# Exponentials of three heads on ScalarE, of the fourth on VectorE as weighted 16-bit linear pieces; a new normalization and out-projection

## The chip, the cores and the metric

The kernel runs on one core of a Trainium2 chip. The metric is the device time of one execution in microseconds (us), lower is better. Each quoted time is a median of several runs. Runs of one kernel that lie over 1.5% above its fastest are set apart as slow, and only fast runs are compared.

The engines are TensorE (PE in the profile, PEld for its weight loads), VectorE (DVE), ScalarE (ACT), GpSimd (POOL) and SyncE (SP), which issues the DMAs. PEclk is the clock granted to TensorE as a fraction of full speed. In the traces it has two values only, 0.5 and 1.0. It changes on a grid of 3.41 us. The Trainium skill, "TensorE: Matmul & The Clock Gate", Part 1: The HAM clock gate, says the same: two states, half and full rate, set by how busy TensorE has been, in windows of 3413 ns.

## The reference

Four layers on 2,048 tokens of width 512. Layers 1 and 3 are a local dilated attention, not touched by the change. Layers 2 and 4 are full attention with 32 query heads of 16 dimensions that share one key and one value head. Cut to what matters:

```python
# x: (1, 2048, 512); H = 32 heads, Dh = 16
q = (x @ wq).reshape(B, S, H, Dh).transpose(0, 2, 1, 3)
k = x @ wk                      # one key head for all
v = x @ wv
scores = einsum("bhqd,bkd->bhqk", q, k) * Dh ** -0.5
p = softmax(scores)             # 2 layers x 32 heads x 2048 x 2048 exponentials
o = einsum("bhqk,bkd->bhqd", p, v)
out = o.transpose(...).reshape(B, S, H * Dh) @ wo
```

## The kernel before

The work of a full-attention layer is cut into chunks: one head, 128 keys, 512 queries. There are 2,048 chunks in a layer, 4,096 in all. Three chunks make a tile. For each tile TensorE computes three score matmuls, ScalarE takes one exponential over 128x1536, and TensorE multiplies the result with the values (PV).

```python
def emit_scores(i):                                   # L498
    for n, (qc, t, a, kt, g) in enumerate(cs):        # cs: three chunks
        nc.tensor.matmul(st[:, n, :], lhsT=KAB[32*g:32*g+32, a, kt*128:(kt+1)*128],
                         rhs=QT[32*g:32*g+32, t, qc*512:(qc+1)*512],
                         start=True, stop=True, tile_position=(32*g, 0))     # L503
def emit_exp(i):
    nc.scalar.activation(out=pt[...], in_=st[...], func=AF.Exp, scale=scale) # L511
def emit_pv(i):
    ...
        nc.tensor.matmul(o_ps[...][32*g:32*g+32, :], lhsT=VE[:, kt, :], rhs=pt[:, n, :],
                         start=(kt == 0), stop=(kt == NT-1),
                         tile_position=(0, 32*g))                            # L547
```

A score matmul uses 32 rows of the array (its contraction is 32 long), and a PV matmul uses all 128 rows and 32 columns. So consecutive groups use different tilings of the array. A group of matmuls in different row groups or column groups runs at nearly the same time (in the traces they start within 10 ns of each other); I call that one stream.

VE holds the values with a column of ones beside them, so a PV matmul also sums the exponentials. When the 16 key tiles of a block (four heads, 512 queries) are done, VectorE copies the block out, spreads the sums with a shuffle, takes a 128x512 reciprocal and multiplies; four output matmuls and four additions follow for every block.

```python
def finish_block(qc, t, a):
    nc.vector.tensor_copy(out=ot[:], in_=ops[:])
    nc.vector.stream_shuffle(out=lb[:, sl], in_=ot[:, sl], mask=[16] * 32)   # L535
    nc.vector.reciprocal(out=lb[:, sl], in_=lb[:, sl])                       # L536
    nc.vector.tensor_tensor(out=onb[:, sl], in0=ot[:, sl], in1=lb[:, sl], op=ALU.mult)
    ...  # later, four times: y = onb x wo_pad (L520), x_sb += y (L521)
```

## Time and profile before

| | before |
|---|---|
| median time, as known before the result | 2388.58 us (3 runs, 2383.91 to 2392.66) |
| from first to last exponential, two attention stages | 955.2 + 956.3 us |
| ScalarE busy in attention | 97% |
| one exponential of 128x1536, start to start | 1.331 us median, 1.40 us mean |
| granted TensorE clock in attention | 0.50 |
| VectorE busy in attention | 25 to 32% |

The page of the profile shows the span in 40 slices, each digit being the busy share of a slice in tenths; PEclk is the granted clock in tenths. These are the rows of TensorE, ScalarE and the clock in the kernel before.

```profile
PE   5887899999999999999877879999999989999996
...
ACT  5314999999999999999842169999999999999996
...
PEclk9998555555555555555589975555555555555555
```

The two attention stages are the two long stretches in which ScalarE shows 9. In both of them the clock is 5, half speed. The costliest groups of the kernel before are next. Each line gives source line, engine, operation, result and operands, shapes and count, then busy time in us, the mean of one in ns, and the idle time before them with the engine that ended it.

```profile
L511 ACT ACTIVATE pt<-st 128x1536 bf16<-128x1536 f32 (+1 forms) x1366 | 1860.7, 1508 | 63.9 <-PE st L503 62.0
L503 PE MATMUL st<-QT,KAB 32*128 32x512 bf16 x4096 | 859.4, 597 | 176.1 <-ACT pt L511 168.2
L547 PE MATMUL o_ps<-pt,VE 128*32 128x512 bf16 x4096 | 864.7, 607 | 1.4 <-ACT pt L511 1.0
...
L536 DVE RECIPROCAL lb<-lb 128x512 f32<-128x512 f32 (+1 forms) x70 | 214.9, 3075 | 2.1
```

ScalarE is busy 1,861 us with exponentials and idle only 64 us before them: it bounds these stages. Before score matmuls TensorE waits 168 us for ScalarE; ScalarE waits 62 us for TensorE. (One exponential is listed at 1.5 us, but consecutive ones overlap and start 1.33 us apart.) The busy time by stretches of time (columns: busy us of PE, PEld, DVE, ACT, POOL with counts, then PEclk, DMA share, GB/s) gives the shares in a steady part of attention.

```profile
300.00:400.00 100.00, 91.22 (x446) 21.76 (x444) 26.36 (x30) 97.25 (x73) 0.00 (x0) 0.50 0.00 1
```

In 100 us there are 73 exponentials. The PE column, 91%, is not the array at its peak: it contains the latency of each group. The timeline of the same kernel (columns: start us, duration us, instruction, count) shows how often groups can follow each other.

```profile
901.34 0.61 PE L547 MATMUL o_ps<-pt,VE 128*32 128x512 bf16 x3
901.52 2.79 ACT L511 ACTIVATE pt<-st 128x1536 bf16<-128x1536 f32 x2 [0.17 <-PE st L503]
...
901.89 0.61 PE L503 MATMUL st<-QT,KAB 32*128 32x512 bf16 x3
...
902.43 0.61 PE L547 MATMUL o_ps<-pt,VE 128*32 128x512 bf16 x3
```

PV group, score group and PV group start 0.54 to 0.55 us apart, so the two groups of a tile take 1.09 of ScalarE's 1.33 us at half clock. TensorE has little to spare there.

### The profile page before, as it was taken

To read this page: it belongs to the slowest core of one execution; us is meant where nothing else is said; L and a number is where in the kernel's file an instruction comes from. 1 tells how busy PE (TensorE), PEld (TensorE's weight loads), DVE (VectorE), ACT (ScalarE), POOL (GpSimd) and SP (SyncE) were. 2 spreads that over 40 slices of the span, in tenths; PEclk is the share of its full clock that TensorE was granted. 3 is DMA by queue.
4 is the path that set the end of the run, shared out by engine and by line. 5 is a ranking of instruction groups with operands and counts; after the bars stand their busy time and mean duration, and the time that the engine had idled before them with its cause. 6 is when DMAs were issued, how large, how long until landed. Compare 5 with 4: busy or idle time off the path is not lost.

```text
span 2389.7 us, 27720 instructions
## 1 busy us (share of the span) xinstructions
PE 2085.2 (87%) x11652; PEld 611.5 (26%) x11652; DVE 839.2 (35%) x1061; ACT 2015.7 (84%) x1603; POOL 35.7 (1%) x67
## 2 busy tenths in 40 slices
PE   5887899999999999999877879999999989999996
PEld 5433222222222222222153332222222222222221
DVE  3875222232223222322339832222222222222222
ACT  5314999999999999999842169999999999999996
POOL 1002000000000000000010000000000000000000
PEclk9998555555555555555589975555555555555555
DMA  1101000000000000000000000000000000000000
GB/s 63 37 2 28 1 1 1 1 1 1 1 1 1 1 1 1 1 1 1 1 3 2 1 1 1 1 1 9 1 1 1 1 10 1 1 9 1 1 1 11
DMA packets 14315, 11.56 MB, mean 5 GB/s; under 512 B 7904, under 2 KB 13536, under 8 KB 14048
## 3 DMA queue, kind: packets, MB, share of 16 engines
q1 hardware_dynamic: 13120, 8.60, 1.4%
q8 instruction: 95, 1.56, 0.3%
q10 hardware_dynamic: 1056, 1.05, 0.1%
q14 instruction: 44, 0.36, 0.1%
HBM read 7.37 MB, written 2.10 MB: 4 GB/s over the span
## 4 chain that ended last, share of the span: by engine, by line
ACT 39%; PE 31%; issue 17%; DVE 12%; POOL 0%; DMA 0%; ACTq 0%; SPq 0%; DVEq 0%; POOLq 0%
ACT pt L511 38%; PE st L503 11%; PE o_ps L547 8%; PE y L520 6%; DVE lb L536 3%; PE ps L184 3%; DVE prod L209 2%; PE y L265 1%; PE ps L359 1%; DVE pv L253 1%; PE acc L256 1%; DVE ot L528 1%; DVE lb L535 1%; DVE onb L537 1%; DVE qsq L373 0%
## 5 line engine op out<-in xcount | busy, mean ns | idle before, releaser
L511 ACT ACTIVATE pt<-st 128x1536 bf16<-128x1536 f32 (+1 forms) x1366 | 1860.7, 1508 | 63.9 <-PE st L503 62.0
L503 PE MATMUL st<-QT,KAB 32*128 32x512 bf16 x4096 | 859.4, 597 | 176.1 <-ACT pt L511 168.2
L547 PE MATMUL o_ps<-pt,VE 128*32 128x512 bf16 x4096 | 864.7, 607 | 1.4 <-ACT pt L511 1.0
L528 DVE COPY ot<-o_ps 128x512 f32<-128x512 f32 x64 | 44.3, 692 | 1163.2 <-PE o_ps L547 1163.2
L503 PEld LDWEIGHTS <-KAB 32*128 32x128 bf16 x4096 | 236.5, 99 | 766.1 <-issue 764.0
L547 PEld LDWEIGHTS <-VE 128*32 128x32 bf16 x4096 | 154.4, 101 | 621.4 <-issue 621.3
L521 DVE TENSOR_TENSOR x_sb<-x_sb,y 128x512 f32<-128x512 f32 x256 | 176.1, 688 | 226.1 <-PE y L520 226.1
L536 DVE RECIPROCAL lb<-lb 128x512 f32<-128x512 f32 (+1 forms) x70 | 214.9, 3075 | 2.1
L520 PE MATMUL y<-wo_pad,onb 128*128 128x512 bf16 x256 | 155.3, 607 | 20.6 <-DVE onb L537 12.3
L89 ACT ACTIVATE xn<-x_sb,ln_nmr,ln_rstd 128x512 bf16<-128x512 f32 x44 | 33.3, 806 | 92.0 <-DVE ln_nmr L83 88.8
L209 DVE TENSOR_TENSOR prod<-Qch,Kch 128x4096 bf16<-128x4096 bf16 x32 | 72.4, 2279 | 58.1 <-ACT Kch L188 56.7
L184 PE MATMUL ps<-xnT,w_sb 128*32 128x512 bf16 x1536 | 90.7, 392 | 1.9 <-ACT Vch L188 1.9
L184 PEld LDWEIGHTS <-w_sb 128*32 128x32 bf16 x1536 | 80.1, 141 | 12.1 <-issue 7.5
L256 PE MATMUL acc<-pv,ident 128*128 128x512 bf16 x256 | 68.7, 402 | 15.9 <-DVE pv L253 10.3
L212 PE MATMUL lg<-prod,ident 128*128 128x512 bf16 x256 | 60.6, 379 | 18.8 <-DVE prod L209 18.8
L258 ACT CAST Och<-acc 128x2048 bf16<-128x2048 f32 x8 | 14.9, 1866 | 72.2 <-PE acc L256 72.2
L253 DVE TENSOR_TENSOR pv<-attn,Vch 128x2048 bf16<-128x2048 bf16 x64 | 73.2, 1222 | 1.5 <-PE acc L256 1.5
L214 ACT ACTIVATE L<-lg 128x512 f32<-128x512 f32 x16 | 9.6, 598 | 70.7 <-PE lg L212 70.7
L99 PE MATMUL pT<-ident,xn 128*128 128x128 bf16 x256 | 27.6, 256 | 44.6 <-ACT xn L89 29.8
L520 PEld LDWEIGHTS <-onb 128*128 128x128 bf16 x256 | 26.4, 103 | 131.6 <-issue 89.7
L535 DVE STREAM_SHUFFLE lb<-ot 128x512 f32<-128x512 f32 (+1 forms) x70 | 46.8, 673 | 0.0
L537 DVE TENSOR_TENSOR onb<-ot,lb 128x512 bf16<-128x512 f32 (+1 forms) x70 | 44.6, 641 | 2.1
(89 smaller groups left out, 538.8 us busy)
## 6 DMA issues: line engine op xcount, KB each, us to landing
xi<-in_A_x_dram SPq DMA_DIRECT2D x4, 512.0 KB, 5.6
wo_r_73<-in_A_wo_dram SPq DMA_DIRECT2D x4, 512.0 KB, 8.2
w_sb<-in_A_wqkv_dram SPq DMA_DIRECT2D x4, 384.0 KB, 8.2
out_dram<-xo SPq DMA_DIRECT2D x2, 512.0 KB, 3.0
out_dram<-xo ACTq DMA_DIRECT2D x2, 512.0 KB, 4.9
wq_sb<-in_B_wq_dram SPq DMA_DIRECT2D x4, 128.0 KB, 3.2
woB_sb<-in_B_wo_dram SPq DMA_DIRECT2D x4, 128.0 KB, 3.7
wo_pad<-in_B_wo_dram SPq DMA_DIRECT2D x16, 32.0 KB, 1.8
```

The source lines that it names most:

```text
L184: nc.tensor.matmul(ps[32 * c:32 * c + 32, :], lhsT=wqkvP[:, kt, j, d, :], rhs=xnT[:, kt, c * 512:(c + 1) * 512], start=(kt == 0), stop=(kt ...
L209: nc.vector.tensor_tensor(out=prod[:], in0=Q[:, dsl, :], in1=K[:, dsl, PAD - DIL * w:PAD - DIL * w + 512], op=ALU.mult)
L253: nc.vector.tensor_tensor(out=pv[:], in0=attn[:, w, :].unsqueeze(1).to_broadcast([PCH, DG, 512]), in1=V[:, ds_, PAD - DIL * w:PAD - DIL * ...
L256: nc.tensor.matmul(acc[:, i, :], lhsT=ident[:PCH, :PCH], rhs=pv[:, i, :], start=(w == 0), stop=(w == W - 1))
L503: nc.tensor.matmul(st[:, n, :], lhsT=KAB[32 * g:32 * g + 32, a, kt * 128:(kt + 1) * 128], rhs=QT[32 * g:32 * g + 32, t, qc * 512:(qc + 1) ...
L511: nc.scalar.activation(out=pt[:, :len(cs), :], in_=st_tiles[i][:, :len(cs), :], func=AF.Exp, scale=scale)
L520: nc.tensor.matmul(y[:], lhsT=onb[:, cols], rhs=wo_pad[:, t, a, :], start=True, stop=True)
L521: nc.vector.tensor_tensor(out=x_sb[:, qt, :], in0=x_sb[:, qt, :], in1=y[:], op=ALU.add)
L535: nc.vector.stream_shuffle(out=lb[:, sl], in_=ot[:, sl], mask=[16] * 32)
L536: nc.vector.reciprocal(out=lb[:, sl], in_=lb[:, sl])
L537: nc.vector.tensor_tensor(out=onb[:, sl], in0=ot[:, sl], in1=lb[:, sl], op=ALU.mult)
L547: nc.tensor.matmul(o_ps[(qc, t, a)][32 * g:32 * g + 32, :], lhsT=VE[:, kt, :], rhs=pt[:, n, :], start=(kt == 0), stop=(kt == NT - 1), tile ...
```

## The change

The intent is to take a quarter of the exponentials off ScalarE. A step is now one key tile for four heads (1,024 steps). Three heads go through the exponential of ScalarE as before. The fourth head, a different one in each key tile, goes to VectorE:

- A first instruction (L523, "fix") turns its scores from PSUM into 16-bit integers, scaled so that the integer is a logarithm to the base 2.
- A bfloat16 number whose bits are taken as an integer is nearly a logarithm of its value: adding a constant and reading the integer's bits as bfloat16 gives 2 to that power, with straight pieces between the powers. One such curve is a coarse exponential. Four copies, shifted by about a quarter of a power each and added with weights, are a finer one.
- Each copy is one 16-bit pass of VectorE over four key tiles at once (L528), so one pass per step. The weighted sum costs VectorE nothing: PE makes it, with four weighted copies of the values. PV rises from 4 to 7 matmuls a step.

The normalization goes too. The sums of two blocks are gathered by DMA into 128x32, VectorE takes one small reciprocal, DMAs spread it through DRAM, and GpSimd multiplies (L582). Two blocks are packed so that the output projection is four matmuls and one addition for each 128 queries, done once per 512 queries, where it had been done once per block. Not shown below: the bound on the scores up to which this fast path is taken falls from 50 to 42 (`SAFE_EXP_ARG`). The diff, cut to its core (cuts marked with ...):

```diff
+J_OFF = (-0.375, 31.125, 62.875, 95.375)
+J_W = (1.0, 0.84375, 0.71875, 0.60546875)
+T_SCALE = 512.0 * 1.4426950408889634 * DH ** -0.5
+T_BIAS = -1057.4609391288138
...
-    VE = big.tile([128, NT, 32], BF16, name="VE")
+    VE = big.tile([128, NT, NJ, 32], BF16, name="VE")     # values times J_W[j]
...
+    dvp = ctx.enter_context(tc.tile_pool(name=f"Bf_dv_{tag}", bufs=1, space=PSUM))
...
+    def emit_scores(s):                                   # gd = kt % 4 goes to VectorE
+        st = st_tiles[s] = stp.tile([128, 3, 512], F32, name="st")
+        dv = dv_tiles[s] = dvp.tile([128, 512], F32, name="dv")
...
+    def emit_fix(s):
+        nc.vector.tensor_scalar(out=t_tiles[m][:, r, :], in0=dv_tiles.pop(s)[:], scalar1=T_SCALE,
+                                scalar2=T_BIAS, op0=ALU.mult, op1=ALU.add)
+    def emit_pass(m, j):
+        nc.vector.tensor_scalar(out=it[:].bitcast(I16), in0=t_tiles[m][:], scalar1=0.25,
+                                scalar2=127.0 * 128.0 + J_OFF[j], op0=ALU.mult, op1=ALU.add)
+    def emit_pv_act(s):       # three matmuls with VE[:, kt, 0, :]
+    def emit_pv_dve(m, j):    # four matmuls, heads r at key tiles kt0 + r, with VE[:, kt, j, :]
...
-        nc.vector.stream_shuffle(...); nc.vector.reciprocal(lb 128x512); nc.vector.tensor_tensor(onb)
+        nc.sync.dma_start(out=S2[32*g:32*g+32, a, :], in_=src[32*g+16:32*g+17, :])   # 4 times
+        nc.vector.reciprocal(out=S2[:], in_=S2[:])                                   # 128x32
+        rd (DRAM) <- S2 (4 DMAs), lb <- rd broadcast (8 DMAs)
+        nc.gpsimd.tensor_tensor(out=onc[qc][:, t, :], in0=X[:], in1=lb[:], op=ALU.mult)
```

The score of the fourth head has one PSUM bank (`bufs=1`): the next one can't be computed before VectorE has converted the last.

## The prediction

> **What bounds it now.** The two attention stages run from 230 to 1198 us and from 1414 us to the end, about 1,940 of 2,390 us (timeline). In them ScalarE is 97% busy (busy time by 100-us windows): 1,366 exponentials of 128x1536 take 1,860.7 us (costliest groups), one per 1.34 us in steady state. TensorE waits for it, but not by much: a group of three score or PV matmuls occupies 0.54 us from start to start (timeline), of which I take 0.43 us as streaming and 0.11 us as the change between the two tilings; so 1.09 of 1.34 us. Its granted clock is 0.50 through both stages. VectorE is 28% busy.
>
> **What changes.** Per step (one key tile, four heads; 1,024 steps):
> - ScalarE: one 1536-wide exponential instead of 1.33. Floor 1,024 x 1.345 = 1,377 us, 460 us less than 1,366 x 1.345.
> - VectorE: one PSUM conversion of 128x512 (the 512-wide PSUM copy took 0.69 us) and one 16-bit pass over 2,048 elements. No pass of that form is in the trace; a 16-bit copy of 512 took 0.29 us, which fits the 4x rate that the Trainium skill, "VectorE: DVE Perf Modes", The perf-mode tier table, gives for 16-bit tensor_scalar in SBUF. Estimate: 0.69 us. Back-to-back instructions overlap by about 0.07 us, so 1.25 to 1.38 us. The 3.35-us reciprocals and three quarters of the output additions go. Per-block copies and additions bring VectorE to about 1,400 us: level with ScalarE.
> - TensorE: PV rises from 4 to 7 matmuls a step. I counted the compiled order: the fourth head's score is one matmul into a single PSUM bank, and in more than a third of the steps it sits among the PV matmuls. That gives 2.8 changes of tiling and 4.0 serial streams a step: 2.04 us at clock 0.5, but 1.18 us at full clock. **The clock decides.**
>
> **The clock.** Attention streams about 64% of the time at clock 0.5 and never leaves it. Elsewhere (granted clock in 3.4-us windows) dense matmuls raise it after one full window, VectorE-bound stretches at about 56 to 75% of full-clock streaming keep it, and windows under 40% lose it. The change streams about 85% at half clock, then about 59% at full clock: I expect it to rise and mostly stay, with drops at block ends. The shakiest step.
>
> **Sum.** Outside attention: 450 us, plus about 6 for the extra V copies. Attention at full clock: ScalarE, VectorE and the single-buffered PSUM bank (score, convert, score) couple to about 1.45 us a step, 1,485 us; block ends (copy, four output matmuls, the pause of PV) about 40; two tails through four DMA hops, about 12 us each, little more than now. About 2,005 us; some stretches at half clock make it 2,030. Fully at half clock it would be about 2,600.
>
> Predicted **2030 us, 1930 to 2270**. Faster by over 2%: 0.83; within 2%: 0.04; slower: 0.13.
>
> **What would show it.** Right: exponentials x1024 at about 1.5 us mean duration, ScalarE still over 88% busy in attention; VectorE over 85% busy, passes near 0.69 us; granted clock mostly 1.0 in attention; PV matmuls x7168. Wrong on the clock: 0.5 throughout, TensorE near 100% busy, ScalarE idle before exponentials waiting on scores, steps near 2 us. Wrong on VectorE: passes of 1.2 us or more, ScalarE waiting while VectorE is full.
>
> **What would make it wrong.** A low clock; passes off the 4x rate; the single PSUM bank turning every VectorE delay into a TensorE stall.

## The result, and the profile after

| | before | after |
|---|---|---|
| median, fast runs | 2386.57 us (4 runs, 2383.91 to 2392.66) | 1968.18 us (4 runs, 1960.04 to 1973.17) |
| ratio | | 0.824 (95% interval 0.822 to 0.827) |
| first to last exponential, both stages | 1911.5 us | 1470.9 us |
| the rest of the span | 478.2 us | 487.4 us |
| mean granted clock | 0.583 | 0.971 |

A ratio, here and below, is the mean time of one kernel's fast runs over that of the other's in the same rounds, so it isn't quite the ratio of the medians. The last three rows are of the profiled runs (spans 2389.7 and 1958.3 us). The gain of 431 us between those two is 441 us won in the attention stages and 9 us lost around them.

The rows of the page that answer to those of before:

```profile
PE   5888799999999999989678888999999999999995
...
DVE  4797589999999999999638966999999999999995
ACT  5232599999999999999652236999999999999994
...
PEclk9999799999999999999889997999999999999998
```

ScalarE and VectorE are now both at 9 in attention, and the clock is 9 (nearly full) instead of 5. The groups after:

```profile
L517 ACT ACTIVATE pt<-st 128x1536 bf16<-128x1536 f32 x1024 | 1413.8, 1461 | 69.8 <-PE st L511 42.6
L523 DVE TENSOR_SCALAR tt<-dv 128x512 int16<-128x512 f32 x1024 | 700.8, 684 | 107.3 <-PE dv L511 96.2
L528 DVE TENSOR_SCALAR it<-tt 128x2048 int16<-128x2048 int16 x1024 | 699.6, 700 | 7.4
L536 PE MATMUL o_ps<-it,VE 128*32 128x512 bf16 x4096 | 648.0, 387 | 1.7 <-DVE it L528 1.5
L536 PE MATMUL o_ps<-pt,VE 128*32 128x512 bf16 x3072 | 513.9, 393 | 1.8 <-DVE xo L595 0.7
L511 PE MATMUL st<-QT,KAB 32*128 32x512 bf16 x3072 | 434.8, 390 | 32.3 <-ACT pt L517 26.2
```

The exponentials fell from 1,861 to 1,414 us of busy time, and they still wait only 70 us. The 16-bit pass takes 0.70 us for four times the elements that the fix handles in 0.68 us. A matmul now lasts 0.39 us where it had lasted 0.60 us. The busy time by stretches, first in the steady part and then at the start of the first attention stage:

```profile
300.00:400.00 100.00, 94.41 (x792) 21.44 (x788) 93.53 (x151) 98.51 (x73) 2.54 (x2) 1.00 0.05 10
...
236.00:244.00 8.00, 8.00 (x46) 1.34 (x39) 5.63 (x9) 5.54 (x5) 0.00 (x0) 0.50 0.00 0
244.00:250.00 6.00, 5.55 (x53) 1.42 (x47) 4.44 (x8) 5.76 (x5) 0.00 (x0) 0.87 0.00 1
250.00:260.00 10.00, 8.66 (x74) 2.19 (x74) 8.17 (x14) 10.00 (x8) 0.00 (x0) 1.00 0.01 2
```

From 236 to 244 us the clock is still 0.50: TensorE is busy all 8 us, ScalarE 5.5 of 8, and exponentials come about every 2.07 us (in the timeline four steps lie between the starts at 235.36 and 243.62 us). From 245 us the clock is full, and ScalarE is full too. After that, the first stage has a single 3.4-us window at half clock (at 655 us) and the second, full from 1218 us on, has none until its end. So the start of each stage, before the clock rises 18 to 24 us after the first exponential, shows what a whole stage would be without it. The first four steps are short (1.36 us), because the PV matmuls of VectorE's pieces begin only at 233.0 and 1199.9 us; after them, nine steps of the second stage (1199.83 to 1217.54 us) took 1.97 us each in the mean. Over both stages the exponentials start 1.436 us apart on average and 1.348 us in the median.

One visible disturbance is left in steady state, in the timeline of the kernel after:

```profile
430.30 1.27 POOL L582 TENSOR_TENSOR onc<-X,lb 128x512 bf16<-128x512 f32 x1 [42.11 <-DMA lb<-rd]
430.43 1.68 DVE L528 TENSOR_SCALAR it<-tt 128x2048 int16<-128x2048 int16 x1
...
434.11 2.79 ACT L517 ACTIVATE pt<-st 128x1536 bf16<-128x1536 f32 x2 [0.83 <-PE st L511]
```

While GpSimd multiplies, the VectorE pass takes 1.68 instead of 0.70 us, and shortly after ScalarE waits 0.83 us. The Trainium skill, "SBUF — State Buffer", Who interferes with whom, says that a VectorE copy or tensor_scalar in a two-port mode and a GpSimd instruction lock the shared pair of SBUF ports against each other for a whole instruction. This trace agrees: the pass ends 0.54 us after GpSimd's instruction, nearly a whole pass later. It is so for the whole trace: of 24 passes that started during one of the 32 products, 23 ended 0.55 us after it, and the 11 fixes that started during one, which read PSUM, took their usual 0.68 to 0.69 us.

### The profile page after: what moved, and what is told of

It is laid out like the page before. It is cut to its first block, busy times and chain, and to the rows that moved or that the text cites. A ratio compares the mean times of both kernels' runs of the same rounds, so it can differ in the third digit from the quotient of the medians.

```text
span 1958.3 us, 35782 instructions
## 1 busy us (share of the span) xinstructions
PE 1737.2 (89%) x14596; PEld 520.2 (27%) x14596; DVE 1672.4 (85%) x2657; ACT 1569.1 (80%) x1261; POOL 76.0 (4%) x104
## 4 chain that ended last, share of the span: by engine, by line
DVE 44%; PE 41%; issue 6%; ACT 4%; SPq 2%; DMA 2%; POOL 1%; DVEq 0%; POOLq 0%; ACTq 0%
DVE tt L523 18%; DVE it L528 16%; PE o_ps L536 15%; PE dv L511 9%; PE st L511 7%; PE ps L194 3%; ACT pt L517 2%; DVE prod L219 2%; PE y L275 2%; SPq L566 1%; PE ps L364 1%; DVE pv L263 1%; DVE ln_stats L89 1%; PE acc L266 1%; DVE X L559 1%
## 5 line engine op out<-in xcount | busy, mean ns | idle before, releaser
L517 ACT ACTIVATE pt<-st 128x1536 bf16<-128x1536 f32 x1024 | 1413.8, 1461 | 69.8 <-PE st L511 42.6
L523 DVE TENSOR_SCALAR tt<-dv 128x512 int16<-128x512 f32 x1024 | 700.8, 684 | 107.3 <-PE dv L511 96.2
L528 DVE TENSOR_SCALAR it<-tt 128x2048 int16<-128x2048 int16 x1024 | 699.6, 700 | 7.4
L536 PE MATMUL o_ps<-it,VE 128*32 128x512 bf16 x4096 | 648.0, 387 | 1.7 <-DVE it L528 1.5
L536 PE MATMUL o_ps<-pt,VE 128*32 128x512 bf16 x3072 | 513.9, 393 | 1.8 <-DVE xo L595 0.7
L511 PE MATMUL st<-QT,KAB 32*128 32x512 bf16 x3072 | 434.8, 390 | 32.3 <-ACT pt L517 26.2
L511 PE MATMUL dv<-QT,KAB 32*128 32x512 bf16 x1024 | 390.0, 381 | 59.1 <-DVE tt L523 47.4
L511 PEld LDWEIGHTS <-KAB 32*128 32x128 bf16 x4096 | 151.6, 91 | 584.8 <-issue 583.0
L582 POOL TENSOR_TENSOR onc<-X,lb 128x512 bf16<-128x512 f32 x32 | 42.0, 1312 | 1467.2 <-DMA lb<-rd 920.9
L589 PE MATMUL o_ps<-woB_sb,onc 128*128 128x512 bf16 x112 | 31.3, 400 | 28.2 <-POOL onc L582 25.7
```

The costliest lines, as they stand in the source:

```text
L511: nc.tensor.matmul(out, lhsT=KAB[32 * g:32 * g + 32, a, kt * 128:(kt + 1) * 128], rhs=QT[32 * g:32 * g + 32, t, qc * 512:(qc + 1) * 512], ...
L517: nc.scalar.activation(out=pt[:], in_=st_tiles.pop(s)[:], func=AF.Exp, scale=scale)
L523: nc.vector.tensor_scalar(out=t_tiles[m][:, r, :], in0=dv_tiles.pop(s)[:], scalar1=T_SCALE, scalar2=T_BIAS, op0=ALU.mult, op1=ALU.add)
L528: nc.vector.tensor_scalar(out=it[:].bitcast(I16), in0=t_tiles[m][:], scalar1=0.25, scalar2=127.0 * 128.0 + J_OFF[j], op0=ALU.mult, op1=ALU ...
L536: nc.tensor.matmul(o_ps[b][32 * g:32 * g + 32, :], lhsT=VE[:, kt, j, :], rhs=rhs, start=(b, g) not in started, stop=stop, tile_position=(0 ...
L582: nc.gpsimd.tensor_tensor(out=onc[qc][:, t, :], in0=X[:], in1=lb[:], op=ALU.mult)
```

## The experiments

The twelve kernels of the experiments all gave correct results. Labels that begin with b change the kernel before, those with a (and after_order) the kernel after. The texts give the ideas numbers and letters; the sections below say each one in words. In short: the prediction's theory is that a quarter fewer exponentials on ScalarE give the gain, and that TensorE can follow only because the added PV matmuls bring its full clock. The rivals were that the clock alone gives the gain, that the new normalization does, and that TensorE's clock hardly matters after the change.

| run | median us | ratio to before (95%) | mean clock, profiled run |
|---|---|---|---|
| after | 1968.18 | 0.824 (0.822 to 0.827) | 0.971 |
| b_scores2 | 2722.93 | 1.140 (1.138 to 1.142) | 0.572 |
| b_norm | 2354.70 | 0.986 (0.985 to 0.988) | 0.597 |
| b_pv3 | 2333.13 | 0.976 (0.974 to 0.978) | 0.980 |
| a_oldnorm | 2799.77 | 1.171 (1.168 to 1.174) | 0.683 |
| a_pe3 | 2931.41 | 1.228 (1.225 to 1.230) | 0.973 |
| a_nj2 | 2076.87 (2038.63 to 2082.69) | none, see there | 0.782 |
| a_nj2_it2 | 1977.03 | 0.827 (0.825 to 0.828) | 0.926 |
| a_spread | 1948.33 | 0.815 (0.814 to 0.817) | 0.949 |
| a_onc | 1968.58 | 0.824 (0.823 to 0.825) | 0.967 |
| a_spread_onc | 1934.28 | 0.809 (0.808 to 0.811) | 0.962 |
| after_order | 2011.06 | 0.841 (0.835 to 0.846) | 0.942 |
| a_order | 1949.98 | 0.815 (0.812 to 0.818) | 0.945 |

Versions are compared across batches by their ratios to the kernel before. Differences of 14 to 29 us below are given because the intervals of the ratios do not overlap.

### b_scores2: does any streaming raise the clock?

The kernel before with every score matmul computed twice into the same place. TensorE then streams more of the time, without another byte of PV.

```diff
-        for n, (qc, t, a, kt, g) in enumerate(cs):
+        for n, (qc, t, a, kt, g) in list(enumerate(cs)) * 2:
             nc.tensor.matmul(st[:, n, :], lhsT=KAB[...], ...)
```

> The kernel before, with every score matmul issued twice (same result), to raise the clock alone. Theory 1 (ScalarE's count of exponentials is the gain; TensorE only has to keep up): streaming at half clock would be 3 x 0.43 of about 1.5 us per tile, about 85%, so the granted clock should rise to 1.0, and the time falls by no more than the 63.9 us that ScalarE idled before exponentials: 2320 to 2390 us. Rival A (the higher clock itself is the gain): 2240 us or less. If the clock stays at 0.5, each tile takes about 1.5 us and the run is near 2550 us.

Measured: 2722.93 us, 14% slower. The clock did not rise. For that case about 2550 us had been expected; the exponentials came 1.51 us apart in the median, as expected, but 1.64 us in the mean. The clock row of its page, its exponentials, and two groups of its timeline:

```profile
PEclk9996555555555555555589965555555555555555
```

```profile
L511 ACT ACTIVATE pt<-st 128x1536 bf16<-128x1536 f32 (+1 forms) x1366 | 1979.7, 1450 | 278.7 <-PE st L503 207.4
L503 PE MATMUL st<-QT,KAB 32*128 32x512 bf16 x8192 | 1439.0, 616 | 7.1 <-DVE flags L399 5.4
```

```profile
400.19 1.04 PE L503 MATMUL st<-QT,KAB 32*128 32x512 bf16 x6
...
401.15 0.61 PE L547 MATMUL o_ps<-pt,VE 128*32 128x512 bf16 x3
...
401.70 1.03 PE L503 MATMUL st<-QT,KAB 32*128 32x512 bf16 x6
```

A tile takes 401.70 - 400.19 = 1.51 us of TensorE without a pause, and TensorE, at half clock, became the bound (ScalarE waits 279 us). By my count of the trace, matmuls of any kind stream 83% of each 3.41-us window here, against 84% in the windows before the clock rises in the kernel after. So the share of time in which TensorE streams, the prediction's criterion, doesn't decide the clock by itself. What streams must matter too, and the next run tries the other kind.

### b_pv3: do PV matmuls raise it, and what is the full clock worth alone?

The kernel before with every PV matmul three times (the sums grow by three as well, so the quotient is unchanged).

```diff
+        for run in runs:                      # chunks of one block
+            for rep in range(3):
+                for n, (qc, t, a, kt, g) in run:
                     nc.tensor.matmul(o_ps[...], lhsT=VE[:, kt, :], rhs=pt[:, n, :],
-                             start=(kt == 0), stop=(kt == NT - 1), ...)
+                             start=(kt == 0 and rep == 0), stop=(kt == NT - 1 and rep == 2), ...)
```

> The kernel before, with every PV matmul three times (sums and denominators tripled, same result). The runs so far suggest that the granted clock follows the time in which 128-row operands stream (PV), and that 32-row score matmuls count for much less. Here PV would stream about two thirds of the time at half clock, so the clock should rise to 1.0 and stay. Theory 1 (a full clock alone is worth at most ScalarE's idle): 2320 to 2385 us at granted clock above 0.9. Rival A (the clock itself is the gain): 2240 us or less. If the clock stays at 0.5: near 2.1 us per tile, over 3200 us.

Measured: 2333.13 us, with three times the PV work 2.4% faster than before. The clock is full through attention:

```profile
PEclk9998999999999999999979989999999999999998
```

```profile
L511 ACT ACTIVATE pt<-st 128x1536 bf16<-128x1536 f32 (+1 forms) x1366 | 1840.7, 1656 | 30.6 <-PE st L503 26.7
```

Two things follow. PV matmuls do raise the clock where score matmuls did not. And with the full clock at 1,366 exponentials, net of what the tripled PV matmuls cost, the gain is 2.4%, some 56 us, of the 418 us: the exponentials come every 1.360 instead of 1.400 us on average. The rival that the clock by itself gives the gain is refuted: ScalarE is 99% busy in the stretches of steady attention.

### b_norm: the new normalization and out-projection alone

The kernel before with the new `finish_block` and `emit_y` of the change, and nothing else of it.

```diff
-            nc.vector.stream_shuffle(...); nc.vector.reciprocal(...); nc.vector.tensor_tensor(...)
+        for g in range(4):
+            nc.sync.dma_start(out=S2[32*g:32*g+32, a, :], in_=src[32*g+16:32*g+17, :])
+        ...      # the rest as in the change: rd, lb, product on GpSimd, emit_y with four matmuls
```

> The kernel before, with only the new normalization and output projection; all exponentials stay on ScalarE. Theory 1: 256 single output matmuls of 0.54 us become 128 in groups of four, so at most the 63.9 us of ScalarE idle are won, and the tails cost some 10 us: 2330 to 2390 us, clock still 0.5. Rival B (the new normalization and projection bring a large part of the 420 us): 2280 us or less.

Measured: 2354.70 us, 1.4% faster, about 33 us. The clock is 0.516 in the mean over attention: it rises six times, each time after a window with output matmuls, now four in a row, and is lost again 10 us later. ScalarE waits 41 instead of 64 us:

```profile
L506 ACT ACTIVATE pt<-st 128x1536 bf16<-128x1536 f32 (+1 forms) x1366 | 1840.1, 1614 | 41.0 <-PE st L498 40.9
```

Alone, this part is worth little, because VectorE and the output matmuls had not been the bound. The rival that the normalization gives the gain is refuted for the kernel before. No run adds both, full clock and new normalization, to the kernel before; but at the median spacing of 1.331 us its 1,366 exponentials alone take 1,818 us, so by this estimate both together could win at most some 93 of the 1911.5 us of attention, where the change won 441. Next comes the question whether the change could do without it.

### a_oldnorm: the change without the new normalization

The kernel after with the old shuffle, 128x512 reciprocal and product on VectorE. The packed out-projection stays.

```diff
-        (gathering of sums, 128x32 reciprocal, DRAM hop, product on GpSimd)
+        nc.vector.tensor_copy(out=ot[:], in_=ops[:])
+        nc.vector.stream_shuffle(out=lb[:], in_=ot[:], mask=[16] * 32)
+        nc.vector.reciprocal(out=lb[:], in_=lb[:])
+        nc.vector.tensor_tensor(out=onb[:], in0=ot[:], in1=lb[:], op=ALU.mult)
+        for g in range(4):
+            nc.sync.dma_start(out=onc[qc][32*g+16*a:32*g+16*a+16, t, :], in_=onb[32*g:32*g+16, :])
```

> The changed kernel, but with the old normalization on VectorE (shuffle, 512-wide reciprocal and product, each block), the new projection kept. It adds about 0.65 + 3.3 + 0.6 us of VectorE per block, 64 times, about 290 us. Theory 1 (VectorE, 94% busy in attention, limits together with ScalarE, so the new normalization is a precondition): 2170 to 2270 us, ScalarE idle rising by about as much. Rival C (ScalarE at 96% is the only bound, VectorE has slack): 2020 us or less.

Measured: 2799.77 us, 17% slower than before, and far outside the expectation of 2170 to 2270 us. The clock, the chain of work that ended last and the exponentials:

```profile
PEclk9997775757575765555589977666765567557555
...
PE 68%; DVE 13%; ACT 11%; issue 8%; POOL 0%; DMA 0%; SPq 0%; ACTq 0%; DVEq 0%; POOLq 0%
...
L517 ACT ACTIVATE pt<-st 128x1536 bf16<-128x1536 f32 x1024 | 1440.6, 1452 | 883.4 <-PE st L511 652.8
```

The clock falls 49 times in the two attention stages, where the kernel after has a single fall within them. Steps at full clock (383 of them) took 1.70 us in the mean, steps at half clock (639) took 2.59 us. If all had taken 1.70 us, the time would be about 1022 x 1.70 + 503 us outside attention, 2,240 us, inside the expectation. The other 639 x (2.59 - 1.70) = 570 us are steps at half clock. So the added VectorE work was costed about right, as far as the steps at full clock, which are not a random choice, can show. What was missed is that VectorE's stalls (a 3.35-us reciprocal per block) come with gaps in the PV stream (34 of the 49 falls follow a window with over 0.5 us of a reciprocal in it), that the clock is lost in windows with such gaps (PV streams 15% of the window before a fall, 37% where the clock stays full), and that TensorE is then too slow to catch up. The new normalization is worth 1.4% alone and is what keeps the change from being a loss.

### a_pe3: how close is TensorE to the bound after the change?

The kernel after with every score and PV matmul three times.

```diff
-        for g, out in outs:
+        for g, out in outs * 3:
...
-        for n, g in enumerate(g for g in range(4) if g != gd):
+        for n, g in list(enumerate(g for g in range(4) if g != gd)) * 3:
...
+        for rep in range(3):
             for r in range(4):
```

> The changed kernel with every score and PV matmul three times (sums and denominators both tripled, so the result is the same). Counted in its compiled order: 1.9 changes of tiling and 9.1 streams a step, 2.16 us a step at full clock, about what the unchanged order would cost at half clock (2.04). Theory 1 (the win depends on the clock having risen): 2600 to 2720 us at granted clock 1.0, slower than the kernel before. Rival D (TensorE has so much slack that the clock does not matter): under 2050 us.

Measured: 2931.41 us, where 2600 to 2720 us had been expected. The step is 2.336 us in the median where 2.16 was expected, so the size missed upward; ScalarE waits 965 us, and the clock is full (0.973). TensorE's work is therefore a bound as soon as it grows, even at full clock. The rival that its clock hardly matters after the change is refuted: at half clock the steps of the kernel after took 1.97 to 2.07 us at the start of a stage (shown above), which over 1,024 steps would be 0.53 to 0.63 us x 1,024, an estimated 550 to 650 us more.

### a_nj2 and a_nj2_it2: less work, and the clock

If the clock hangs on PV matmuls, a version with fewer of them should be in danger. a_nj2 takes two linear pieces instead of four: half as many VectorE passes, and 5 instead of 7 PV matmuls a step.

```diff
-J_OFF = (-0.375, 31.125, 62.875, 95.375)
-J_W = (1.0, 0.84375, 0.71875, 0.60546875)
+J_OFF = (0.0, 64.02)
+J_W = (1.0, 0.70703125)
-T_BIAS = -1057.4609391288138
+T_BIAS = -541.66
...
+        j -= 4 - NJ          # the two passes sit in the last two of four steps
```

> The changed kernel with two linear pieces in place of four: VectorE loses half of its passes, TensorE 2 of 11 matmuls per step. Theory 2 (the clock follows PV streaming, which falls to 5 matmuls a step): the clock stays at or drops to 0.5 for most of attention, each step then costs TensorE about 1.68 us, and the run takes 2080 to 2260 us, slower than the changed kernel although it does less. Rival E (the clock follows any TensorE work, or less work is simply faster): 1860 to 1930 us.

Measured: 2076.87 us in the median, at the lower edge of the expected 2080 to 2260; one run at 2038.63, the other three, the profiled one among them, near 2080 and slow for that. So there is no ratio of fast runs, and the runs are read by their clock histories. The clock row and one stretch of the profiled run:

```profile
PEclk9999655567986997898689995555589779968986
```

```profile
300.00:400.00 100.00, 99.33 (x500) 15.51 (x494) 58.08 (x88) 80.00 (x56) 1.46 (x2) 0.50 0.03 5
```

With VectorE at 58% and the clock at 0.50, TensorE is busy 99% and ScalarE 80%: the first stage began with 188 us at half clock, the second with 273 us (390 and 425 us at half clock in all). Steps at full clock took 1.335 us in the mean, steps at half clock 1.808 us. Even its fastest run (clock 0.804; the others 0.770 to 0.782) is slower than the kernel after with twice the passes. A kernel with strictly less work lost because TensorE did not get its clock.

a_nj2_it2 is a_nj2 with each piece multiplied twice at half weight: more matmuls, no other work.

```diff
-T_BIAS = -541.66
+T_BIAS = -541.66 - 512.0
...
+        for rep in range(2):
             for r in range(4):
                 pv(b, r, kt0 + r, j, it[:, r, :], ...)
```

> Two pieces as in the run before, but each PV matmul of a piece issued twice, at half its weight: TensorE does as many matmuls as in the changed kernel, VectorE half of the passes. Theory 2: the clock is as high as in the changed kernel, VectorE has slack, and ScalarE alone bounds: about 1.36 us x 1,024 + 40 + 440, so 1850 to 1910 us; 280 us or so under the run with the same pieces and fewer matmuls. Rival E: the extra matmuls cost or change nothing, so no faster than that run.

Measured: 1977.03 us, 100 us faster than a_nj2's median, and 62 us faster than its one fast run, with 2,048 more matmuls. The clock came back to 0.926, still with many drops of one window. But the expected 1850 to 1910 us was missed: with a quarter of VectorE's work gone it is no faster than the kernel after. Part of this is the lower clock (0.926 against 0.971), but the steps at full clock too took 1.413 us in the mean, where those of the kernel after took 1.428. So VectorE's fullness (94%) can't be the main thing that kept the kernel after from ScalarE's floor.

### a_spread, a_onc and a_spread_onc: bursts and the product

In a_nj2_it2 eight PV matmuls of pieces come in each of two steps and none in the two others. a_spread puts four into each step, with one pass in every second step.

```diff
-    def emit_pv_dve(m, j):
+    def emit_pv_dve(m, step):
-        it = i_tiles.pop((m, j))
-        for rep in range(2):
-            for r in range(4):
+        j = step // 2
+        it = i_tiles[(m, j)] if step % 2 == 0 else i_tiles.pop((m, j))
+        for r in range(4):
...
-        if 0 <= m < nsteps // 4 and j >= 0:
-            emit_pass(m, j)
+        if 0 <= m < nsteps // 4 and r % 2 == 0:
+            emit_pass(m, r // 2)
```

> Two pieces at half weight, each PV matmul of a piece twice, as in the last run but one, but spread so that every step has four of them, as in the changed kernel; VectorE has one pass in every second step. TensorE does the same work at the same places as in the changed kernel, VectorE half of the passes. Theory 3 (the last run won nothing because two steps in four had no PV of pieces, so single windows lost the clock): granted clock in attention back to about 0.98, ScalarE alone bounds, 1.36 to 1.38 us a step: 1860 to 1920 us. Rival F (the steps are set by the single-buffered score-convert chain and TensorE's order, not by VectorE's load): 1945 to 1985 us, as the changed kernel.

Measured: 1948.33 us, 29 us better than a_nj2_it2 and 20 us better than the kernel after. The expected 1860 to 1920 us was missed again; the rival range, 1945 to 1985, holds it. Steps take 1.426 us in the mean, 1.330 in the median, 1.402 in the mean at full clock. So spreading helps, and bursts are not the main part of the missing 0.1 us.

a_onc moves the 32 GpSimd products of the kernel after to VectorE, eleven steps later, when their data has long come. a_spread_onc does the same to a_spread.

```diff
-        nc.gpsimd.tensor_tensor(out=onc[qc][:, t, :], in0=X[:], in1=lb[:], op=ALU.mult)
+        late.append((now[0] + 11, onc[qc][:, t, :], X, lb))
...   # in the loop, once now has reached the number:
+            nc.vector.tensor_tensor(out=out, in0=X[:], in1=lb[:], op=ALU.mult)
```

> The changed kernel with the 32 products of normalization on VectorE in place of GpSimd, issued 11 steps after the block. In the trace of the changed kernel a VectorE pass that met such a product took 1.68 us in place of 0.69, and ScalarE idled 0.83 us after it. If that block of VectorE by GpSimd is what it costs, the product itself (about 0.62 us on VectorE, 32 times 20 us in all) takes less than it frees (32 times about 1 us): 0 to 20 us faster. If VectorE's load is what counts: up to 20 us slower.

> The first two edits of this batch together: half of the passes, spread, and the product on VectorE, which has slack now. Theory 3: 10 to 25 us below the first run of this batch, so 1845 to 1905 us. Rival F: within 10 us of it.

Measured: a_onc 1968.58 us over five rounds, no difference from the kernel after (ratio 0.8242 against 0.8243, from different rounds). a_spread_onc 1934.28 us, 14 us under a_spread: the difference is as expected (10 to 25 us), the absolute 1845 to 1905 us was missed. So avoiding the visible lock, 1.68 us for a pass, wins nothing when VectorE itself takes the product at 94% busy, and some 14 us where VectorE has room (72% of the span). The product also comes eleven steps later; that was not tried by itself. a_spread_onc is the fastest version and beats both kernels, 19% under before. It passed the same comparison with the reference; how its two pieces compare in accuracy with four was not measured beyond that. Its clock row and groups:

```profile
PEclk9999889999999999999979997999999999999997
...
L516 ACT ACTIVATE pt<-st 128x1536 bf16<-128x1536 f32 x1024 | 1396.0, 1485 | 54.9 <-PE st L510 27.4
L522 DVE TENSOR_SCALAR tt<-dv 128x512 int16<-128x512 f32 x1024 | 704.1, 688 | 329.2 <-PE dv L510 303.5
```

### after_order and a_order: the scattered score matmuls

In the compiled order the fourth head's score matmul often sits alone among the PV matmuls (the prediction counted that), which costs changes of tiling. The next idea was that these cost the rest. Both kernels force all four scores of a step ahead of the PV matmuls that follow in the program.

```diff
+            last_score[0] = nc.tensor.matmul(out, lhsT=KAB[...], ...)
...
+        i = nc.tensor.matmul(o_ps[b][32*g:32*g+32, :], lhsT=VE[:, kt, j, :], rhs=rhs, ...)
+        order_after(tc, i, last_score[0])
```

> The changed kernel with one edit: the compiler may no longer put the fourth head's score among the PV matmuls; all four scores of a step go first. Same instructions; counted in the compiled order, 1.96 changes of tiling and 3.5 streams a step in place of 2.81 and 4.0, so 0.97 us of TensorE a step at full clock in place of 1.17. The steps of the changed kernel have a median of 1.35 us and a mean of 1.44. Theory 4 (what is left over 1.35 us is TensorE catching up after block ends): 1900 to 1945 us. Rival G (it is VectorE and the single score bank; TensorE now stops for each late conversion, the order was there to hide that): 1965 to 2020 us.

> The same edit on the fastest version so far (half of the passes, spread, and the product on VectorE; 1934 us). VectorE has slack there, so the fourth score seldom waits. Theory 4: 1870 to 1915 us, with the granted clock in attention still above 0.9, since PV streams 0.43 of 1.35 us. Rival G: 1930 us or more. If the clock is lost at half clock with a shorter step (1.70 us), over 2000 us.

Measured: after_order 2011.06 us, 43 us slower than the kernel after; a_order 1949.98 us, 16 us slower than a_spread_onc. The groups of after_order:

```profile
L519 ACT ACTIVATE pt<-st 128x1536 bf16<-128x1536 f32 x1024 | 1413.7, 1457 | 120.3 <-PE dv L513 60.9
L525 DVE TENSOR_SCALAR tt<-dv 128x512 int16<-128x512 f32 x1024 | 702.2, 686 | 159.3 <-PE dv L513 147.9
```

TensorE's busy time fell from 1737 to 1675 us, as the idea had it, but VectorE idles 159 instead of 107 us before fixes and ScalarE 120 instead of 70 us before exponentials. The clock has a part in it: it falls 17 times within the stages, not once, and stands at half for 153 instead of 45 us. But the steps at full clock are longer too, 1.470 instead of 1.428 us in the mean. That fits the rival: the score that goes to VectorE has one bank, it can be computed only once VectorE has converted the last one, and PV matmuls kept behind it wait with it. The scattered order hides that wait. In these two kernels the changes of tiling are cheaper than what they avoid.

### How the clock follows the matmuls

From the traces of all fourteen kernels I took each 3.41-us window of the attention stages, the share of it in which matmuls of any kind stream, the share in which matmuls with 128 rows (PV, and the few output matmuls) do, and the clock of the next window. A stream of 512 columns is counted as 0.43 us at half clock and 0.22 us at full clock: groups that follow each other without a change of tiling start 0.43 us apart in the output projection of layer 1 at half clock (before, from 163.6 us) and 0.22 us apart in the repeated PV of b_pv3 at full clock. Windows close to a limit fall to either side of it when these lengths change by a hundredth. These are the windows at half clock: how many there were, and after how many of them the clock rose.

| any matmul | 128 rows under 0.48 | 128 rows 0.48 to 0.55 | 128 rows over 0.55 |
|---|---|---|---|
| 0.80 to 0.85 | 718, rose 0 | 196, rose 30 | 74, rose 15 |
| 0.85 to 0.90 | 209, rose 0 | 74, rose 28 | 114, rose 101 |
| over 0.90 | 1, rose 0 | 2, rose 2 | 26, rose 26 |

At the same total, the clock rises only after windows with about half of their time in 128-row streams; b_scores2 makes up most of the first column of numbers but is not needed for it (without it they are 231 and 46, and none rose). At full clock, no fall followed any of 3,611 windows with 128 rows at 0.30 or more and a total of 0.40 or more, and 113 followed the 193 windows with 128 rows under 0.25 and a total of 0.40 to 0.60. In the kernel before, 128-row matmuls stream 0.37 of a window; in the kernel after 0.56 just before the rise and then, at full clock, 0.38. That what streams matters is also shown by intervention, in b_scores2 against b_pv3.

But it is not the single matmul's 32 rows that count for less. In the kernel before, outside attention, the window from 163.4 us at half clock holds nothing but 32-row matmuls, four at a time in the four row groups (the output projection of layer 1), and the clock rises after it:

```profile
163.28 15.03 PE L265 MATMUL y<-wo_r_73,Och 32*128 32x512 bf16 x244 [1.95 <-ACT Och L258]
...
163.40:166.81 3.41, 3.41 (x36) 1.55 (x32) 0.00 (x0) 0.00 (x0) 0.00 (x0) 0.50 0.03 5
166.81:170.22 3.41, 3.41 (x68) 1.86 (x64) 1.54 (x3) 0.00 (x0) 0.00 (x0) 1.00 0.00 0
```

There are 17 such windows, over 0.90 full, in twelve of the traces, and the clock rose after each. The score groups of the kernel before and of b_scores2 have only three at a time. So I counted rows in use together: every instant of a window weighs 1 for a 128-row matmul and a quarter for each 32-row matmul that streams then (others in proportion). Over all windows of all fourteen traces, in and outside attention, the clock rose after 227 of the 228 half-clock windows over 0.78 and after 3 of the 2,106 under 0.70; at full clock it was lost after none of 5,499 windows over 0.40 and after all 139 under 0.30. In attention the kernel before has 0.60 in the mean, b_scores2 0.71 (0.75 at most), b_pv3 0.79 and 0.81 in its two windows before a rise. This one count fits the attention stages and the rest; it is inferred from the traces, and no run was made to test it.

## Why the prediction was right or wrong

The prediction was 2030 us (1930 to 2270), and the time is 1968.18 us: the direction and the range held, 62 us under the middle.

- **ScalarE's floor.** Right. 1,024 exponentials at 1.345 us were predicted as 1,377 us; the median spacing is 1.348 us, and ScalarE is 94 to 99% busy in the stretches of steady attention. b_pv3 shows that before this cut a full clock of TensorE won only 2.4%, and ScalarE's own spacing allowed an estimated 93 us at most.
- **The costs on VectorE.** Right. The pass was taken from the Trainium skill, "VectorE: DVE Perf Modes", The perf-mode tier table, as 0.69 us; it took 0.70 us, and the fix 0.68 us. VectorE is 91 to 95% busy in the stretches of steady attention.
- **TensorE at half clock would cost 2.04 us a step.** Right, and seen directly, though in few steps: 2.07 us at the start of the first stage (four steps), 1.97 us in the second (nine).
- **The clock would rise and mostly stay.** The outcome was right, the criterion was not. "Streams about 85% at half clock ... I expect it to rise" would also have made b_scores2 rise (83%), and it stayed at 0.5. What rose in the change, along with the total, is the share of 128-row streams, from 0.37 to 0.56 of a window, and so the rows in use, from 0.60 to 0.78. The prediction was lucky in that the change added just those matmuls. The same weakness made me expect 2170 to 2270 us of a_oldnorm, which took 2800.
- **Attention.** 1,485 + 40 us for block ends were predicted, and 25 more for stretches at half clock; first to last exponential is 1,471 us, those stretches included. This is the mis-sized term: 79 us too much. Steps with block ends and half clock took 1.436 us, where 1.45 us was taken before either.
- **Outside and the tails.** 456 + 2 x 12 = 480 us predicted, 487 us measured. But the parts missed in opposite directions: from the last exponential to the last addition of the first stage it is about 23 us (11 before), not 12, as SyncE issues the four groups of DMAs one behind the other (965.9 to 976.5 us, before a product at 978.1 us); the rest was shorter than thought. "Little more than now" failed.
- **The sum.** 79 - 7 = 72 us too much against the profiled run of 1958 us, 62 against the median.

Not settled: what the rest of a step above ScalarE's 1.33 us is, 0.07 us in a_spread_onc (1.405 us mean) and 0.1 us in the kernel after. VectorE's fullness, bursts of PV, GpSimd's product and the order of scores were each tried, and none alone explains it. In a_nj2, with 5 PV matmuls a step, the steps at full clock took 1.335 us, block ends included, while a_spread, with the same VectorE work and 7, took 1.402 us. That points to TensorE's load, but a_nj2's full clock is a chosen half of its steps, and a second bank for VectorE's scores was not tried.

## What to carry to other kernels

When a change shifts the bound from one engine to three that are nearly level, find out first which clock TensorE will get: in this case the same step took about 2 us at half clock and 1.35 us at full clock, and two kernels ran slower than themselves with useless matmuls added (before against b_pv3, a_nj2 against a_nj2_it2). Count how many rows are in use together, not only how long TensorE streams, and see what opens gaps; giving the old normalization back to VectorE cost 832 us, 570 of them in steps at half clock. A part of a change that is worth 1.4% alone can be what the rest of it needs, so undo parts from the changed kernel as well as adding them to the old one.

## What the Trainium skill lacked or had wrong

- "TensorE: Matmul & The Clock Gate", Part 1: The HAM clock gate, lets the clock follow from how busy TensorE is. It does not say that the rows in use count: in b_scores2 TensorE was busy without a pause (1.51 us per tile, 83% of each window streaming, but with three 32-row matmuls at a time in its score groups) and the clock stayed at 0.5 through both attention stages, while b_pv3 with repeated 128-row matmuls had it full, and outside attention windows full of 32-row matmuls, four at a time, raised it. It also gives no level of activity in a window at which the full clock is kept; here it was lost after none of 5,499 windows with over 0.40 of the rows in use, and after all 139 under 0.30.
- "TensorEngine Tiling (Array Packing)", Key Properties, says that changing the tiling mode drains TensorE, but gives no cost. Here groups of one stream alternating between two tilings started 0.54 us apart at half clock and 0.32 us at full clock, of which about 0.11 and 0.10 us is more than the streaming (0.43 and 0.22 us, as counted above).
- "VectorE: DVE Perf Modes", The perf-mode tier table, lists 2,048 elements of bf16 at 693 ns for tensor_scalar. The table does not list int16, though the page's rules for the modes speak of 16-bit types in general; the int16 pass of 2,048 elements took 0.70 us here, the same.
- "SBUF — State Buffer", Who interferes with whom, was right: a pass of 0.70 us took 1.68 us while GpSimd multiplied for 1.27 us.
